# A conv-plus-linear-attention kernel: merged parameter loads, a shorter exponent matrix, a later zero-fill, and a new table for the order

## The chip, the cores and the metric

The kernel runs on one core of one Trainium2 chip. The metric is the device time of one execution in microseconds, lower is better. Engines are named as in the profile: TensorE (PE, with its weight loads as PEld), VectorE (DVE), ScalarE (ACT), GpSimd (POOL) and SyncE (SP), which here issues all DMAs.

## The reference

Two independent heads work on 2048 positions and 576 channels in float32; their results are joined along the last axis.

```python
# head A: long convolution with a kernel made of 128 damped waves per channel
dt = exp(log_dt);  A = -exp(log_A_real) + 1j * A_imag;  C = (C_real + 1j * C_imag) * dt[:, None]
P = exp((A * dt[:, None])[:, :, None] * pos)                  # (576, 128, 2048)
K = 2 * einsum("dn,dnl->dl", C, P).real                       # (576, 2048)
y = irfft(rfft(u.T, 4096) * rfft(K, 4096))[:, :2048].T + u * D_skip

# head B: linear attention, 32 heads of 18, with a learned feature map
q, k, v = split(x @ wqkv)
pq, pk = q @ w_phi, k @ w_phi                                 # per head
phi = lambda p: concat(softmax(p), softmax(-p))               # 36 features
o = phi(pq) @ (phi(pk).T @ v) / (phi(pq) @ sum(phi(pk)) + 1e-6)
b = o.reshape(2048, 576) @ wo
out = concat(y, b)
```

## The kernel before

**Head B.** 16 tiles of 128 positions. A key tile (`key_tile`) is three float32 products split into high and low parts (42 matmuls of 378 or 396 columns), a double softmax (`softmax`) and the keys-times-values product (32 matmuls `ps<-e,v`), which accumulates over the 16 tiles in `kvt`. The first of these products, of whichever tile comes first in the order, writes the mark `opened`; the others read it. After the last one the result is written into a block diagonal: `kvb` (126 x 1330) is cleared by GpSimd (L636) and stored to the DRAM buffer `kz` (L637), the 18 x 18 blocks are stored over it (L652), and the whole is loaded back into `kvb` (L655). Before that, `kvb` serves as a stage for one piece of the key weights. A query tile (`query_tile`) has a query product in two halves of 14 matmuls of 288 columns, softmax, ten transposes, the division (`ps<-kvb,fT`), transposes and the output product, again in two halves. The weights of keys and values are folded with `w_phi` on the chip (`fold`, `ps<-fT,e`), then those of queries (`fold` again) take their place.

**Head A.** 36 groups of 16 channels, done in pairs, in six blocks of six. For a block, `params` loads the step size `dt` (in `ldt`), the frequencies `th` and the two parts `cre` and `cim` of the coefficients, each 128 x 96, and works out phases in turns; `exponents` loads the block's exponents `mg` from the DRAM buffer `gd`, which `mags` has filled. `gd` holds 64 rows (four kinds times 16 channels). For a group, GpSimd builds integer phases by doubling (L883 to L888), ScalarE makes sines and cosines (L905 to L916), three matmuls with the constant `sel` (`ps<-sel,mg`) make exponents, ScalarE exponentiates them (L930), VectorE multiplies (L936 to L941) and 64 small matmuls (`ps<-E,cs`) give the kernel's rows. `sel` is loaded in three pieces (`sel_part`) through the buffer `v1`, of which there are two and which the key tiles use as well; every group's matmuls wait for all three. `mg` and `sel` have 128 rows: `mg` holds `gd` twice, and `sel` holds zeros where the second copy isn't wanted. Then the kernel (`k_first`, `ps<-ks,w`) and `u` (`u_first`, `ps<-ub,w`) go through a first transform stage to DRAM; 16 `product` steps (`ps<-ub,ff`, `ps<-kb,fk`, `ps<-ac,ff`) multiply them, and 16 `last` steps (`ps<-zi,w`) end the inverse transform.

**The order.** All operations are handed to `Plan.op`, and `Plan.run` writes them out engine by engine. It keeps a modelled time of each engine, and picks among the ready operations by a key: the due time in the table `WANT` (one number per unit, such as a key tile or a group pair), less the `LEAD` of the step. Operations given as `any` or as a pair of engines go to the one that the model has free first. Where the model sees TensorE wait for the first matmul into a fresh PSUM buffer, it writes fillers ahead (products with a zero tile, L215), which keep TensorE busy. SyncE's DMAs stand in one queue in the order of the plan. A `Mark` is a dependency without a buffer. `WANT`, `LEAD` and five weights are numbers in the file.

Of the kernel before, what the change touches and what calls it, by code (L numbers as in the profile page):

```python
# [8 lines left out]
F32 = mybir.dt.float32  # L9
# [13 lines left out]
NG, DG = 36, 4  # L23
# [18 lines left out]
def by_row(x):  # L42

    x = x.reshape(NQ, 4, NG // NQ, DG, -1).transpose(0, 2, 1, 3, 4).reshape(NG, W, -1)
    x = np.concatenate([x, np.repeat(x[-1:], 40 - NG, 0)])
    return np.ascontiguousarray(x.reshape(8, 5, W, -1).transpose(2, 0, 1, 3).reshape(128, -1))


def layouts(i):
    c = np.ascontiguousarray  # L50
    w = i["B_wqkv"]
    wphi = np.zeros((128, 5, 126), np.float32)
    h = 0
# [7 lines left out]
    return dict(  # L61
        u=c(i["A_u"][0].reshape(64, 16, 2, D).transpose(2, 0, 1, 3).reshape(128, 16 * D)), mag=np.stack([by_row(x) for x in (lar, cre, cim)]), ldt2=by_row(i["A_log_dt"][:, None]), aim=by_group(i["A_A_imag"]), cre=by_group(i["A_C_real"]),
        cim=by_group(i["A_C_imag"]), ldt=by_group(i["A_log_dt"][:, None])[0], dsk=c(i["A_D_skip"]),
        xT=twice(i["B_x"][0].T), wv=twice(w[:, 1152:]), wqT=c(twice(w[:, :576]).T), wkT=c(twice(w[:, 576:1152]).T), wphi=wphi,
        wo=twice(i["B_wo"]))


def constants():
# [83 lines left out]
class Mark(Buf):  # L152


    def __init__(self):
        self.tag, self.writers, self.readers = None, [], []


class Plan:
# [26 lines left out]
    def op(self, eng, cost, fn, r=(), w=(), with_=(), early=0.0, table=None, busy=1.0, lock=False, mode=(128, 128), add=None):  # L186
# [10 lines left out]
        for b in w:  # L197
            b.writers.append(k)
        bufs = list({id(b): b for b in (*r, *w, *with_) if not isinstance(b, Mark)}.values())
        for b in bufs:  # L200
# [175 lines left out]
def c_dma(nbytes, run=4096):  # L376
    return nbytes / run * (0.35 + 0.0029 * run)
# [4 lines left out]
FLEX = "dve", "pool"  # L382
STAY, TURNOVER, NEAR, LEAN_POOL, LEAN_ACT = 201.0337, 32.8045, 106.7441, -80.6454, 62.4245
LEAD = dict(g1=-171.8003, g2=572.2435, g3=151.3761, g4=545.6015, k1=48.5812, k2=-375.6500, k3=-757.7275, k4=-640.2771, l1=-1201.2185, p1=-789.5548, p2=-44.7091, p3=-18.2983, p4=-535.3487, q1=82.0847, q2=-177.3983, q3=-254.3079, q4=-403.9251, q5=-398.9575, q6=-829.6788, u1=458.1288, xd=-783.9802)
FILL = 114.0


WANT = dict(
    ident=[-108.8011],
    fold=[-9953.8356, -10398.4174, -453.1777, 165.8967],  # L390
    start=[1616.5931],
    key=[-6472.8031, -3126.8062, -1314.3574, -3125.3684, -656.72, -499.3546, -3140.1215, -1712.5806, -2108.3757,
          -1097.3828, -995.3063, -3475.5769, -5054.2771, -1149.402, -2645.614, -12059.5893],
    kv=[-10.1299],
    query=[5165.3029, 1080.554, 692.3202, 1735.0859, -197.7761, 3588.2092, 2132.912, 435.8626, 2776.5646, 4448.3212,
          4159.3881, 4303.4831, 5219.083, 4714.8471, 4446.1239, 3107.4294],
    u=[-1640.9461, -3267.9218, -4820.103, -2553.3502, -977.4058, -3531.8924, -390.5478, -577.8274, -2654.6962,
          -4160.3913, -2177.6267, -4468.1255, -741.7491, -4170.1538, -4622.046, -4241.0767],
    mags=[-9388.2816],
    sel=[-7210.3842, -4975.1123, -11383.6242],  # L400
    dsk=[2087.7151],
    par=[-11102.6929, -5509.5329, -1199.9769, -424.7275, 1524.2103, 2698.0598],
    group=[-7457.0019, -5406.6149, -4731.1573, -4251.2752, -3514.0599, -2749.8781, -3073.1041, -3256.4294, -3042.7242,
          -2141.1152, -1003.1983, -2662.6797, -315.8551, -156.0662, 211.9443, 4253.1033, 2854.2949, 574.2642],
    kfirst=[-4429.7629, -1297.4347, -385.4741, 1666.6694],
    product=[-90.1674, 1697.6391, -210.3218, 1304.2139, 977.2179, -172.77, 437.5617, -517.2988, 1754.78, 1904.223,
          3993.8576, 2617.1633, 3713.9029, 3193.0326, 3608.0088, 3162.4523],
    last=[2342.2332, 1752.2374, 2676.4796, 653.6455, 734.6483, 754.2121, 126.96, 2202.2106, 3127.1116, 3903.7028,
          3067.4349, 3943.3771, 2944.3536, 3914.8745, 4473.7986, 2888.4515],
)  # L410


def body(tc, nc, i, out, ctx):
# [9 lines left out]

    tags({1: "zero ident w1 w3 hp quarter dsk kvb fT wh wl ks E sel dt th cre cim ax ay mx mn ld ldc",
          2: "v1 o ot pi mg ff ub kb zo us2 ac yo zi", 3: "e fk x9", 4: "cs", 7: "small"})
# [209 lines left out]
    line = lambda: kvb.t.rearrange("p s k g d -> p (s k g d)")  # L635
    op("pool", 1400, lambda: pool.memset(line(), 0.0), w=[kvb])  # L636
    op("sp", c_dma(126 * 5320), lambda: sp.dma_start(flat(), line()), r=[kvb], w=[kz, blank])  # L637
# [127 lines left out]
    pl.at("mags")  # L765
    sel, ld, ldc = B("sel", [128, 1536], F32R), B("ld", [128, 5]), B("ldc", [128, 5])
# [32 lines left out]
    def sel_part(k):  # L799
        st = B("v1", [128, 512])  # L800
        cs = slice(k * 512, k * 512 + 512)
        op("sp", c_dma(128 * 2048), lambda: sp.dma_start(st.t, i["sel"][:, cs]), w=[st])
        copy("act", lambda: sel.t[:, cs], lambda: st.t, [st], [sel], 512)
# [4 lines left out]
    def exponents(blk):  # L808
        mg = B("mg", [128, NG // NB, NS], F32R)
        for h in range(2):  # L810
            op("sp", c_dma(64 * 3072), lambda h=h: sp.dma_start(
                mg.t[64 * h:64 * h + 64].bitcast(F32), gd.t[:, NG // NB * blk:NG // NB * (blk + 1)]), r=[gd], w=[mg])
        return mg

    def params(blk):
        cs = slice(blk * BW, blk * BW + BW)
        dt, th, cre, cim, ax, ay, mx, mn = (B(n, [128, BW]) for n in (
            "dt", "th", "cre", "cim", "ax", "ay", "mx", "mn"))
        tmp, at = dt, ax
        pi, fx = B("pi", [128, 12, BW]), B("ot", [128, 4, BW])  # L820
        op("sp", 300, lambda: sp.dma_start(dt.t, i["ldt"][cs].rearrange("(o d) -> o d", o=1).to_broadcast([128, BW])), w=[dt], early=8)
        for b, n in ((th, "aim"), (cre, "cre"), (cim, "cim")):
            op("sp", 300, lambda b=b, n=n: sp.dma_start(b.t, i[n][:, cs]), w=[b], early=8)

# [294 lines left out]
```

## Time and profile before

| | |
|---|---|
| median of 3 runs | 588.4 us (586.17 to 588.89) |
| profiled execution | 588.28 us, of which the span of the profile is 586.5 us |
| mean granted TensorE clock | 0.991 |
| TensorE busy | 556.6 us (95%) |
| VectorE busy | 513.1 us (87%) |
| ScalarE busy | 389.5 us (66%) |
| GpSimd busy | 251.8 us (43%) |
| DMA | 119.24 MB, queue share 65.1% of 16 engines |

Busy times are of one profiled execution. TensorE's busy time includes the fillers, and its matmuls overlap, so it is no measure of how much work there is.

### The profile page before, as it was taken

The page shows a single profiled execution, that of the slowest core. Times are in us where ns is not written, and L with a number is a line of the kernel's source. Part 1 is how long each engine was busy: PE and PEld are TensorE (multiplying, and loading weights), DVE is VectorE, ACT ScalarE, POOL GpSimd, SP SyncE. Part 2 cuts the span into 40 slices and gives each one's busy share as a digit, 9 for nine tenths or more (in the row PEclk, how much of TensorE's full clock was granted, in tenths as well). Part 3 has the DMA queues.
Part 4 walks back from the last instruction along what each step waited for, and adds up shares of the span by engine and source line. Part 5 has one row for each costly group of instructions (what it writes and reads, how often), then busy time and mean ns, then how long its engine had stood idle before and what let it go on. Part 6 is the DMA issues. An engine that isn't in the chain of part 4 may idle for free.

```text
span 586.5 us, 18741 instructions
## 1 busy us (share of the span) xinstructions
PE 556.6 (95%) x7657; PEld 457.9 (78%) x7657; DVE 513.1 (87%) x1109; ACT 389.5 (66%) x666; POOL 251.8 (43%) x393
## 2 busy tenths in 40 slices
PE   5998999999999899899999999999999999999996
PEld 3998989898879688778888766676788876767884
DVE  5789999999999899799999999799979797777751
ACT  5567767898579978578789777595955444432342
POOL 0448388682383656670566750674300201211000
PEclk9899999999999999899999999999999999999999
DMA  8977521457156767315867466975685799997587
GB/s 250 293 271 233 179 92 45 157 204 253 53 141 205 227 204 212 103 54 128 244 208 209 137 199 163 313 241 160 203 272 180 190 281 305 321 302 253 182 258 207
DMA packets 91316, 119.24 MB, mean 203 GB/s; under 512 B 9826, under 2 KB 73186, under 8 KB 91230
## 3 DMA queue, kind: packets, MB, share of 16 engines
q1 hardware_dynamic: 91230, 118.04, 65.1%
q8 instruction: 60, 0.98, 0.8%
q14 instruction: 26, 0.21, 0.1%
HBM read 68.76 MB, written 49.26 MB: 201 GB/s over the span
## 4 chain that ended last, share of the span: by engine, by line
PE 53%; DVE 24%; DMA 10%; ACT 5%; issue 3%; POOL 2%; SPq 2%; DVEq 0%; ACTq 0%; POOLq 0%
PE ps L431 49%; DVE E L937 3%; DVE e L446 3%; DMA zi<-dram 2%; DVE cs L936 2%; PE ps L678 2%; DMA out_dram<-yo 2%; DVE E L941 1%; DVE E L939 1%; DMA e<-in_wkT_dram 1%; DVE small L580 1%; DVE small L568 1%; PE ps L215 1%; DVE zi L436 1%; DVE e L450 1%
## 5 line engine op out<-in xcount | busy, mean ns | idle before, releaser
L431 PE MATMUL ps<-wh,x 128*128 128x288 f32 (+2 forms) x1008 | 241.8, 320 | 2.5 <-DVE zi L436 1.6
L431 PEld LDWEIGHTS ps<-wh,x 128*128 128x128 f32 x1008 | 174.2, 189 | 14.5 <-issue 6.7
L431 PE MATMUL ps<-wl,x 128*128 128x288 f32 (+2 forms) x560 | 175.5, 314 | 0.0
L888 POOL TENSOR_TENSOR cs<-cs,pi 128x32 int32<-128x32 int32 (+4 forms) x180 | 113.5, 639 | 9.4
L431 PEld LDWEIGHTS ps<-wl,x 128*128 128x128 f32 x560 | 106.4, 190 | 0.7
L579 POOL TENSOR_TENSOR o<-e 128x576 f32<-128x576 f32 x32 | 43.1, 1352 | 98.6 <-ACT e L576 77.1
L930 ACT ACTIVATE ps<-ps 128x512 f32<-128x512 f32 x108 | 56.6, 583 | 10.8 <-PE ps L431 9.7
L431 PEld LDWEIGHTS ps<-kvb,fT 126*128 126x128 f32 (+1 forms) x320 | 39.6, 192 | 8.8 <-issue 2.5
L450 DVE TENSOR_TENSOR ac<-us,ps 128x576 f32<-128x576 f32 x64 | 44.5, 743 | 1.4 <-ACT fT L436 1.1
L431 PE MATMUL ps<-E,cs 128*32 128x64 f32 x2304 | 42.4, 223 | 2.8 <-DVE E L941 1.8
L431 PE MATMUL ps<-kvb,fT 126*128 126x133 f32 (+1 forms) x320 | 42.8, 283 | 1.9 <-ACT fT L436 1.9
L431 PEld LDWEIGHTS ps<-E,cs 128*32 128x32 f32 x2304 | 35.6, 111 | 11.5 <-DVE E L941 4.1
L936 DVE TENSOR_TENSOR cs<-ps,cs 128x1024 f32<-128x1024 f32 x36 | 43.6, 1211 | 1.0 <-ACT ps L930 0.8
L937 DVE TENSOR_TENSOR E<-ps,cs 128x1024 f32<-128x1024 f32 x36 | 43.4, 1207 | 0.1
L446 POOL TENSOR_TENSOR ac<-ac 128x288 f32<-128x288 f32 x19 | 15.3, 805 | 65.2 <-DVE ac L450 65.1
L576 ACT ACTIVATE e<-e 128x1152 f32<-128x1152 f32 x32 | 37.4, 1179 | 5.4 <-POOL e L446 1.9
L436 ACT ACTIVATE ot<-ps 128x288 f32<-128x288 f32 x29 | 11.9, 416 | 40.8 <-PE ps L431 39.8
L912 ACT ACTIVATE cs<-cs 128x1040 f32<-128x1040 int32 x36 | 38.3, 1063 | 0.2
L431 PE MATMUL ps<-sel,mg 128*128 128x512 f32 x108 | 35.4, 428 | 2.8 <-ACT zi L436 1.7
L905 ACT ACTIVATE cs<-cs 128x1040 f32<-128x1040 int32 x31 | 33.1, 1070 | 5.7 <-POOL cs L888 5.7
L916 ACT ACTIVATE cs<-cs,hp 128x1040 f32<-128x1040 f32 x31 | 35.6, 1149 | 0.0
L431 PE MATMUL ps<-kb,fk 128*64 128x288 f32 x256 | 35.4, 414 | 0.1
(141 smaller groups left out, 1058.6 us busy)
## 6 DMA issues: line engine op xcount, KB each, us to landing
xd<-x SPq DMA_DIRECT2D x16, 576.0 KB
dram<-zi SPq DMA_DIRECT2D x16, 576.0 KB
dram<-zi SPq DMA_DIRECT2D x32, 288.0 KB
x<-xd SPq DMA_DIRECT2D x16, 576.0 KB
kb<-dram SPq DMA_DIRECT2D x32, 288.0 KB
ub<-dram SPq DMA_DIRECT2D x32, 288.0 KB
dram<-zo SPq DMA_DIRECT2D x32, 288.0 KB
zi<-dram SPq DMA_DIRECT2D x16, 576.0 KB
```

Source lines behind the costliest of these rows:

```text
L431: pe.matmul(o, l, r, start=start, stop=stop, skip_group_check=skip)
L446: op(eng, [c_dve(n[0]) if e == "dve" else c_pool(n[1]) for e in eng], lambda e: (dve if e == "dve" else pool).tensor_tensor(dst(), a(), b( ...
L450: op(eng, c_dve(n) if eng == "dve" else c_pool(n), lambda: e.tensor_tensor(dst(), a(), b(), op=alu), r=r, w=w, lock=eng == "pool" or not a ...
L576: op("act", c_act(1152) + 40, lambda: act.activation(e.t, e.t, AF.Exp), r=[e], w=[e], table="exp")
L579: op("pool", c_pool(470), lambda: pool.tensor_tensor(pair.t, e.t[:, :, :, 0:9], e.t[:, :, :, 9:18], op=ALU.add), r=[e], w=[pair], lock=True)
L888: op("pool", c_pool(2 * n * W), lambda n=n, j=j: pool.tensor_tensor(x()[:, :, :, n:2 * n], x()[:, :, :, 0:n], pi.t[:, j:j + 2, gs].bitcast ...
L905: act.activation(cs.t[:, 0], x(), AF.Abs)
L912: act.activation(cs.t[:, 1], cs.t[:, 1].bitcast(I32), AF.Sin, scale=TURN)
L916: act.activation(cs.t[:, 0], cs.t[:, 0], AF.Sin, scale=-TURN, bias=hp.t)
L930: op("act", c_act(512), lambda: act.activation(ps.t, ps.t, AF.Exp), r=[ps], w=[ps], table="exp")
L936: op("dve", c_dve(64 * W), lambda: dve.tensor_tensor(F(), both(M.t), F(), op=ALU.mult), r=[M, cs], w=[cs])
L937: op("dve", c_dve(64 * W), lambda: dve.tensor_tensor(E.t[:, :, :, 32:64], both(up.t), cs.t[:, :, :, 0:32], op=ALU.mult), r=[up, cs], w=[E])
```

## The change

1. The four parameter loads of a block become one load of 128 x 384 from an array `four` laid out for it. One buffer (`dt`, one copy) holds all four; `Part` is a mark that stands for a quarter of it, so that each step still waits for its quarter, while the buffer comes free after the last reader of any.
2. `gd` gets eight rows of zeros, written once by a DMA from the zero tile. `mg` and `sel` have 72 rows in place of 128, and a block's exponents are one load in place of two.
3. The memset of `kvb` reads the mark `opened`, so it and its store come after the first keys-times-values product.
4. All numbers of the planner's tables are others, so every engine's order is another. The matmuls other than fillers are the same ones; fillers are 207 in place of 193; ScalarE has 38 table loads in place of 34.

```diff
+    four = np.stack([np.repeat(by_group(i["A_log_dt"][:, None]), NS, 0)] + [by_group(i[x]) for x in ("A_A_imag", "A_C_real", "A_C_imag")])
+    four = c(four.reshape(4, NS, NB, BW).transpose(1, 2, 0, 3).reshape(NS, -1))
...
-    none = np.zeros_like(at)
-    sel = np.concatenate([np.concatenate([at, none, dn], 1), np.concatenate([none, up, none], 1)])
+    sel = np.concatenate([np.concatenate([at, up, dn], 1), np.zeros((8, 1536))])
...
+class Part(Mark):
+    def __init__(self, of, k):
+        super().__init__()
+        self.of, self.k = of, k
+    @property
+    def t(self):
+        return self.of.t[:, self.k]
...
-LEAD = dict(g1=-171.8003, g2=572.2435, g3=151.3761, g4=545.6015, k1=48.5812, ...
+LEAD = dict(g1=-596.9929, g2=367.2719, g3=-490.9828, g4=1181.4843, k1=316.9776, ...
...
-    op("pool", 1400, lambda: pool.memset(line(), 0.0), w=[kvb])
+    op("pool", 1400, lambda: pool.memset(line(), 0.0), r=[opened], w=[kvb])
...
-    gd = B("gd", [4 * W, 40, NS])
+    gd = B("gd", [4 * W + 8, 40, NS])
+    op("sp", 640 * 1.1, lambda: sp.dma_start(gd.t[64:72].rearrange("r g n -> (r g n)").rearrange("(p k n) -> p k n", p=128, k=5),
+                                              pl.zero.t.bitcast(F32)[:, None, :].to_broadcast([128, 5, 64])), r=[pl.zero], w=[gd])
...
-        st = B("v1", [128, 512])
+        st = B("v1", [72, 512])
...
-        mg = B("mg", [128, NG // NB, NS], F32R)
-        for h in range(2):
-            op("sp", c_dma(64 * 3072), lambda h=h: sp.dma_start(
-                mg.t[64 * h:64 * h + 64].bitcast(F32), gd.t[:, NG // NB * blk:NG // NB * (blk + 1)]), r=[gd], w=[mg])
+        mg = B("mg", [4 * W + 8, NG // NB, NS], F32R)
+        op("sp", c_dma(72 * 3072), lambda: sp.dma_start(mg.t.bitcast(F32), gd.t[:, NG // NB * blk:NG // NB * (blk + 1)]), r=[gd], w=[mg])
...
-        op("sp", 300, lambda: sp.dma_start(dt.t, i["ldt"][cs].rearrange("(o d) -> o d", o=1).to_broadcast([128, BW])), w=[dt], early=8)
-        for b, n in ((th, "aim"), (cre, "cre"), (cim, "cim")):
-            op("sp", 300, lambda b=b, n=n: sp.dma_start(b.t, i[n][:, cs]), w=[b], early=8)
+        four = B("dt", [128, 4, BW])
+        dt, th, cre, cim = (Part(four, k) for k in range(4))
+        op("sp", c_dma(128 * 1536, 1536), lambda: sp.dma_start(
+            four.t.rearrange("p k n -> p (k n)"), i["four"][:, 4 * BW * blk:4 * BW * (blk + 1)]), w=[dt, th, cre, cim], early=8)
```

What the new order looks like is shown at three places. First, SyncE's queue at the start of the program, before (`in_sel` is the first third of `sel`, `in_wv` and `in_wkT` are the value and key weights, `in_wphi` the feature map):

```order
L473 DMA zo<-in_xT_dram 128x5x128
L802 DMA v_97<-in_sel_dram 128x512
L821 DMA dt<-in_ldt_dram 128x96
L823 DMA th<-in_aim_dram 128x96
L823 DMA cre<-in_cre_dram 128x96
L823 DMA cim<-in_cim_dram 128x96
L473 DMA zi<-in_wv_dram 128x5x192 x2
L473 DMA cs<-in_wv_dram 128x5x192
L482 DMA fT<-in_wphi_dram 128x630
L486 DMA e<-in_wkT_dram 126x640 x2
```

and SyncE's queue at the same place now:

```order
L836 DMA dt<-in_four_dram 128x384
L487 DMA zo<-in_xT_dram 128x5x128
L487 DMA zi<-in_wv_dram 128x5x192 x2
L487 DMA cs<-in_wv_dram 128x5x192
L496 DMA fT<-in_wphi_dram 128x630
L500 DMA e<-in_wkT_dram 126x640 x2
L500 DMA E<-in_wkT_dram 126x640
```

The first key weights come after six issues in place of ten, and `sel` is no longer ahead of them.

Second, the zeroed block diagonal. GpSimd's queue around its memset before (`pi` are the first block's phases, `v1` a key tile's values, `x9` a key tile's input):

```order
L450 TENSOR_TENSOR pi_133<-pi_133 128x96
L450 TENSOR_TENSOR pi_133<-pi_133 128x192 x2
L636 MEMSET kvb_335 126x1330
L450 TENSOR_TENSOR pi_133<-pi_133 128x192
L615 MEMSET v1_345 128x32
L450 TENSOR_TENSOR pi_133<-pi_133 128x192
L446 TENSOR_TENSOR x9_343<-zo_168,x9_343 64x128
```

GpSimd's queue around it now (`cs_660` are the phases of the fourth group, `o` and `e` belong to a key tile's softmax):

```order
L902 TENSOR_TENSOR cs_660<-cs_660,pi_119 128x16x2x8
L629 MEMSET v1_783 128x32
L650 MEMSET kvb_791 126x1330
L902 TENSOR_TENSOR cs_660<-cs_660,pi_119 128x16x2x16
L593 TENSOR_TENSOR o_882<-e_621 128x576
L464 TENSOR_TENSOR pi_419<-pi_419 128x96
```

and SyncE's queue where its store now stands (`dt` is the third block's parameters, `v1_855` the last third of `sel`):

```order
L496 DMA fT_785<-in_wphi_dram 128x630
L836 DMA dt_801<-in_four_dram 128x384
L651 DMA kz_807<-kvb_791 126x1330
L818 DMA v1_855<-in_sel_dram 72x512
L760 DMA ub_875<-in_u_dram 128x576
L771 DMA dram_394<-zi_849 128x1152
```

The memset has moved from the first block's phases, ahead of all groups, to a place between the fourth group's doublings; the store has moved to the place directly ahead of the last third of `sel`.

Third, TensorE's queue behind the last group's matmuls (`E`), before (`wh` and `wl` are the query and output weights, `ks` the group's result that enters `k_first`):

```order
L431 MATMUL ps_7292<-E_7219,cs_6611 32x64 x32
L431 MATMUL ps_7330<-wh_3090,x9_7222 128x288
L431 MATMUL ps_7330<-wl_3091,x9_7222 128x288
L431 MATMUL ps_7330<-wh_3090,x9_7222 128x288 x2
L431 MATMUL ps_7330<-wl_3091,x9_7222 128x288
L431 MATMUL ps_7330<-wh_3090,x9_7222 128x288 x2
L431 MATMUL ps_7330<-wl_3091,x9_7222 128x288
L431 MATMUL ps_7330<-wh_3090,x9_7222 128x288 x2
L431 MATMUL ps_7330<-wl_3091,x9_7222 128x288
L431 MATMUL ps_7330<-wh_3090,x9_7222 128x288 x2
L431 MATMUL ps_7330<-wl_3091,x9_7222 128x288
L431 MATMUL ps_7350<-ks_5900,w1_253 64x288
```

and TensorE's queue there now (rows with `zero` are fillers, `ident,e` transposes of a query tile):

```order
L445 MATMUL ps_7298<-E_7242,cs_6842 32x64 x32
L229 LDWEIGHTS zero_81
L229 MATMUL ps_7344<-ident_99,zero_81 126x256
L229 LDWEIGHTS zero_81
L229 MATMUL ps_7344<-ident_99,zero_81 126x256
L692 MATMUL ps_7344<-ident_99,e_6703 126x128 x4
L445 MATMUL ps_7353<-ks_6133,w1_210 64x288
```

A half query tile stood behind the last group before; now two fillers and four transposes stand there. From that point to the end 24 such halves, 9 `last` steps and 12 fillers remain, in place of 25, 12 and none.

More of the change, by code (lines that the diff above doesn't have):

```diff
@@ L61, in layouts @@
     return dict(
[L62 to L63 removed]
+        u=c(i["A_u"][0].reshape(64, 16, 2, D).transpose(2, 0, 1, 3).reshape(128, 16 * D)), mag=np.stack([by_row(x) for x in (lar, cre, cim)]), ldt2=by_row(i["A_log_dt"][:, None]), four=four,
+        dsk=c(i["A_D_skip"]),
         xT=twice(i["B_x"][0].T), wv=twice(w[:, 1152:]), wqT=c(twice(w[:, :576]).T), wkT=c(twice(w[:, 576:1152]).T), wphi=wphi,
@@ L198, in op @@
             b.writers.append(k)
-        bufs = list({id(b): b for b in (*r, *w, *with_) if not isinstance(b, Mark)}.values())
+        parts = [b.of for b in (*r, *w) if isinstance(b, Part)]
+        bufs = list({id(b): b for b in (*r, *w, *with_, *parts) if not isinstance(b, Mark)}.values())
         for b in bufs:
@@ L385 @@
+LEAD = dict(g1=-596.9929, g2=367.2719, g3=-490.9828, g4=1181.4843, k1=316.9776, k2=-220.8799, k3=-2198.2025, k4=-520.6920, l1=-811.5782, p1=-279.5317, p2=-417.1315, p3=-485.8669, p4=-415.8287, q1=223.9279, q2=-289.5980, q3=-448.7975, q4=-502.1689, q5=-436.9106, q6=-997.3467, u1=740.1929, xd=-934.5048)
 FILL = 114.0
 WANT = dict(
[L389 to L393, printed above, removed]
@@ L408 @@
-    last=[2342.2332, 1752.2374, 2676.4796, 653.6455, 734.6483, 754.2121, 126.96, 2202.2106, 3127.1116, 3903.7028,
-          3067.4349, 3943.3771, 2944.3536, 3914.8745, 4473.7986, 2888.4515],
+    ident=[1246.8953],
+    fold=[-9373.4449, -11041.9236, -1452.2708, -738.1885],
+    start=[3762.3507],
+    key=[-7908.8211, -3217.3921, -2751.28, -1169.6395, -1541.4876, -1261.3998, -3829.9347, -13218.5904, -3590.9709,
+          -2456.9081, -4376.271, -2454.6704, -1838.419, -2340.4702, -2944.9904, -2655.4107],
@@ L422, in tags @@
                 pl.tag(t, p, n, window)
-    tags({1: "zero ident w1 w3 hp quarter dsk kvb fT wh wl ks E sel dt th cre cim ax ay mx mn ld ldc",
+    tags({1: "zero ident w1 w3 hp quarter dsk kvb fT wh wl ks E sel dt ax ay mx mn ld ldc",
           2: "v1 o ot pi mg ff ub kb zo us2 ac yo zi", 3: "e fk x9", 4: "cs", 7: "small"})
```

40 lines of the change are left out of this document (20 added, 20 removed).

## The prediction

> **What bounds the kernel now.** I read the page first, then the busy time by stretches, then the start, the first group and the end in the timeline. The head of the page:
>
> ```profile
> span 586.5 us, 18741 instructions
> PE 556.6 (95%) x7657; PEld 457.9 (78%) x7657; DVE 513.1 (87%) x1109; ACT 389.5 (66%) x666; POOL 251.8 (43%) x393
> ...
> PE 53%; DVE 24%; DMA 10%; ACT 5%; issue 3%; POOL 2%; SPq 2%; DVEq 0%; ACTq 0%; POOLq 0%
> ```
>
> The third line is the chain that ended last: TensorE holds half of it, VectorE a quarter. The busy times by stretch (start:end, length, then each engine's busy time and its number of instructions, the granted clock, the DMA share and GB/s):
>
> ```profile
> 0.00:30.00 30.00, 22.75 (x141) 20.64 (x142) 18.91 (x52) 16.79 (x31) 8.09 (x24) 0.89 0.92 274
> ...
> 60.00:120.00 60.00, 59.20 (x1094) 54.10 (x1093) 59.17 (x118) 45.30 (x70) 40.70 (x64) 1.00 0.38 121
> 120.00:180.00 60.00, 58.99 (x905) 51.31 (x905) 58.36 (x123) 46.83 (x73) 33.75 (x53) 1.00 0.50 155
> 180.00:225.00 45.00, 41.53 (x741) 34.23 (x738) 41.91 (x100) 40.93 (x67) 26.34 (x41) 1.00 0.71 218
> ...
> 330.00:360.00 30.00, 27.75 (x427) 19.72 (x423) 29.81 (x63) 23.76 (x37) 14.39 (x22) 1.00 0.58 170
> ...
> 453.00:560.00 107.00, 106.28 (x1253) 81.22 (x1253) 83.29 (x198) 40.61 (x93) 16.21 (x15) 1.00 0.84 262
> 560.00:586.50 26.50, 21.27 (x167) 17.37 (x165) 9.03 (x22) 7.66 (x18) 0.00 (x0) 1.00 0.78 236
> ```
>
> Three regimes are to be seen. In the first 30 us the DMA engines are 92% busy and TensorE is not. From 60 to 360 us VectorE and TensorE are both nearly full, so a wait on either shows in the other. From 453 us to 560 TensorE alone is full. 453 us is where the matmuls of the last (36th) convolution group stand:
>
> ```profile
> 453.04 1.10 PE L431 MATMUL ps<-E,cs 128*32 128x64 f32 x64
> ```
>
> The sum is made against the profiled execution's own 588.28 us, 1.8 us over its span and 0.02% below the median of 588.4.
>
> **The change part by part.** Every table of the planner is new, so the order of all engines is new, while the work is almost the same: TensorE has the same matmuls apart from its fillers (207 for 193). I go through the program from its start and cost what differs.
>
> *The first loads.* SyncE's issues (start, duration, issue), the first TensorE work, and the size of one load of `sel` and of one of the four parameters:
>
> ```profile
> 0.74 0.46 SPq L473 DMA_DIRECT2D zo<-in_xT_dram  x1
> 1.26 0.51 SPq L802 DMA_DIRECT2D v<-in_sel_dram  x1
> 1.81 0.43 SPq L821 DMA_DIRECT2D dt<-in_ldt_dram  x1
> ...
> 3.23 0.43 SPq L823 DMA_DIRECT2D cim<-in_cim_dram  x1
> 3.70 1.00 SPq L473 DMA_DIRECT2D zi<-in_wv_dram  x2
> ...
> 6.47 1.15 SPq L486 DMA_DIRECT2D e<-in_wkT_dram  x2
> 14.36 2.05 PE L431 MATMUL ps<-fT,e 126*128 126x126 f32 x8 [5.65 <-DMA e<-in_wkT_dram]
> ...
> v<-in_sel_dram SPq DMA_DIRECT2D x3, 256.0 KB
> dt<-in_ldt_dram SPq DMA_DIRECT2D x6, 48.0 KB
> ```
>
> The first key-weight product waits for its load from 6.47 to 14.36 us. Ahead of that load stand 256 KB of the first third of `sel` and four parameter loads. In the new order the `sel` load is gone from there and the parameters are one load of the same 4 x 48 = 192 KB. At the 274 GB/s of this stretch 256 KB are 0.96 us; the four issues less are (3.70 - 1.26) x 4/5 = 1.95 us. Since the queue is full, the bytes decide: I take -1.0, and keep 0 and -1.95. Cover: if the first product's weights become late for another reason, this gain is gone and costs nothing.
>
> *The parameters.* ScalarE is their first reader, six blocks in all (count | busy, mean ns | idle before, released by):
>
> ```profile
> L827 ACT ACTIVATE ax<-cre 128x96 f32<-128x96 f32 x6 | 1.7, 281 | 4.7 <-DVE pi L450 3.7 <-DMA cre<-in_cre_dram 1.0
> L827 ACT ACTIVATE dt<-dt 128x96 f32<-128x96 f32 x6 | 1.7, 280 | 2.4 <-DMA dt<-in_ldt_dram 2.4
> L827 ACT ACTIVATE ay<-cim 128x96 f32<-128x96 f32 x6 | 1.7, 279 | 0.6 <-DMA cim<-in_cim_dram 0.5
> L431 PE MATMUL ps<-sel,mg 128*128 128x512 f32 x108 | 35.4, 428 | 2.8 <-ACT zi L436 1.7 <-DVE zi L436 0.6 <-ACT v L436 0.5
> ```
>
> ScalarE stood idle 1.0 + 2.4 + 0.5 = 3.9 us for these loads. One load leaves one wait. The merged tile comes free only after its last reader, which is true of `dt` already (it is also the scratch tile), so the wait for `dt` may stay; I take away the other two, -1.5, and keep 0 and -3.9. The 22 SyncE rows fewer and the 56 partitions fewer of `sel` and `mg` I cost at nothing: SyncE's queue is 2% of the chain, and the matmuls of `sel` and `mg` (last row) waited 2.8 us in all, mostly for copies of `zi` and not for a load; if that cover fails it is one issue of about half a microsecond per block.
>
> *The zeroed block diagonal.* Before, it is cleared and stored near 25 us, when GpSimd is nearly idle; now both stand behind the first keys-times-values product. The places there:
>
> ```profile
> 61.62 0.75 PE L431 MATMUL ps<-e,v 128*19 128x36 f32 x64
> 62.41 0.33 SPq L802 DMA_DIRECT2D v<-in_sel_dram  x1
> 65.47 0.63 ACT L439 ACTIVATE sel<-v 128x512 fp32r<-128x512 f32 x1 [0.43 <-DMA v<-in_sel_dram]
> 68.20 0.86 PE L431 MATMUL ps<-sel,mg 128*128 128x512 f32 x3
> ...
> L636 POOL MEMSET kvb<- 126x1330 f32 x1 | 1.2, 1212 | 0.3 <-PE ps L431 0.3
> kz<-kvb SPq DMA_DIRECT2D x1, 654.6 KB
> ```
>
> The last third of `sel` is issued when the first product ends, is copied by 66.1 us, and the first group's matmul comes at 68.20: 2.1 us of slack. Now SyncE issues the 654.6 KB store directly ahead of that load, and the store waits for the memset, which waits for the product. The memset (1.2 us) holds up GpSimd's queue, whose next two rows are the last doubling of a group's phases and a softmax sum. The bytes are 2.4 us at 274 GB/s, and the issue is 0.4 us. Against the slack I charge +0.5; the ends are 0 and 2.4 + 0.4 + 1.2 - 2.1 = +1.9, or all of the first three, +4.0, if the slack is gone. The store that leaves the full DMA queue at 25 us could give up to the same 2.4 us back; I count 0, since 19 fillers (20 before) still stand ahead of the second key product.
>
> *Up to the last group.* Counting each program's rows up to the 36th group and pricing them by their shapes:
>
> ```profile
> L436 DVE COPY zi<-ps 128x288 f32<-128x288 f32 x62 | 25.2, 444 | 4.9 <-PE ps L431 4.7
> L436 ACT ACTIVATE zi<-ps 128x288 f32<-128x288 f32 x66 | 23.2, 421 | 13.1 <-PE ps L431 11.3 <-ACT fT L436 0.9 <-ACT cs L905 0.4
> L912 ACT ACT_TABLE_LOAD x14 | 18.0, 1283 | 0.2
> ```
>
> VectorE has 6 copies of 288 columns fewer (6 x 25.2/62 = 2.4 us) and about 1.1 us less of the rest: -3.5. ScalarE has 15 such copies more (15 x 23.2/66 = 5.3 us), four table loads more (5.1 us) and some 11 us of other work, 21 us in all. VectorE is 97 to 99% busy in 60:180 and 330:360, less elsewhere, so I count half of its 3.5: -1.7 (ends -3.5 and 0). ScalarE has a quarter of its time free before the last group (389.5 - 40.6 - 7.7 = 341 us busy of 453), but carries 5% of the chain: 21 x 5% = +1.0 (ends 0 and the table loads' 5.1).
>
> *After the last group.* Here TensorE is full, so its own rows are the time:
>
> ```profile
> 533.12 0.38 PE L431 MATMUL ps<-wh,x 128*128 128x288 f32 x1
> ...
> 535.15 1.20 PE L431 MATMUL ps<-ub,ff 64*32 64x288 f32 x32
> ...
> 450.00 1.25 PE L678 MATMUL ps<-ident,e 128*126 128x128 f32 x10
> 207.41 1.59 PE L215 MATMUL ps<-ident,zero 128*32 128x256 bf16 x13
> L431 PE MATMUL ps<-zi,w 128*64 128x288 f32 x128 | 18.3, 415 | 1.2 <-DMA zi<-dram 1.1
> ```
>
> In the new order one half-tile query product (2.0 us from 533.12 to 535.15) and three of the 16 last-stage steps (18.3/16 = 1.1 us each) less stand behind the group, one set of transposes (1.25) and 12 fillers (12 x 1.59/13 = 1.5) more: -2.0 - 3.4 + 1.25 + 1.5 = -2.7. This is only won if the work moved ahead found room there; half-sure, I keep 0 as the other end.
>
> *The clock in the middle.*
>
> ```profile
> 240.00:245.00 5.00, 3.77 (x66) 3.64 (x70) 2.23 (x7) 2.36 (x4) 3.28 (x2) 0.68 0.33 115
> 241.23 2.44 PE L431 MATMUL ps<-kvb,fT 126*128 126x133 f32 x12 [1.95 <-ACT fT L436]
> ```
>
> Around the first query division TensorE ran at 0.68 for 5 us, a loss of 1.6 us, after idle pieces of which the longest is 1.95 us. The new order puts 57 fillers (7.0 us) shortly ahead of that division. If they keep the clock up, -1.6; I count 0, because they also occupy TensorE. The Trainium skill, in "TensorE: Matmul & The Clock Gate", Part 1 on the HAM clock gate, has the clock halve only after an idle window of about 3.4 us. By that page this dip should not have come from a 1.95 us gap, and fillers would win nothing there; by the row they could win 1.6 us and the sum would be 581.3. The trace does not agree with the page's window here.
>
> The sum: 588.28 - 1.0 - 1.5 + 0.5 - 1.7 + 1.0 - 2.7 = 582.9 us.
>
> **The rivals.**
>
> *TensorE is the whole bound.* Then what is moved ahead of the last group is paid there, VectorE's gain is idle, and only the start and the 14 fillers more count: 588.28 - 1.0 + 14 x 1.59/13 (1.7) = 589.0. For it: 95% busy. Against it: TensorE's busy time includes 193 fillers, and VectorE holds 24% of the chain.
>
> *ScalarE becomes the bound, slower.* In 180:225 it is busy 40.93 of 45 us, 4.1 us free. By the 18th group (which ends in or shortly after that stretch) the new order has given it about 10.8 us more. If that falls there, the excess of 10.8 - 4.1 = 6.7 us is on the path in place of +1.0, VectorE's 1.7 is idle, and the last group comes late, so that the 2.7 us at the end are lost: 588.28 - 1.0 - 1.5 + 0.5 + 6.7 = 593.0. It decides from more than 4.1 us of added ScalarE work within that stretch. Against it: the work is added over 250 us, most of which have a quarter free.
>
> *The store delays the first group.* The full +4.0 in place of +0.5: 582.9 + 3.5 = 586.4. For it: the store, the memset and the load form a line on one queue. Against it: more `u` products now lie before the first group and can fill the gap.
>
> **How the numbers follow.** The forecast has 0.50 (its own range, by its bounds, 577 to 588), TensorE alone 0.18, ScalarE 0.22, the store 0.10. The low end: all good bounds, 588.28 - 1.95 - 3.9 - 3.5 - 2.7 - 1.6 = 574.6, is reached only together; I take 576. The high end is the slower rival and a little, 594. A measurement of this kernel can tell about 0.5%, 2.9 us, from no change: faster is under 585.4, slower over 591.3. Faster: 0.43 of the forecast's 0.50, 0.03 of TensorE's, 0.02 of ScalarE's and 0.03 of the store's, 0.51. Slower: 0.18 of ScalarE's, 0.05 of TensorE's and 0.04 of the store's and the forecast's together, 0.27. Same: 0.22.
>
> **What would show it.** Right: the first key-weight product near 13.4 us instead of 14.36; no wait for `cre` or `cim` on ScalarE; the first group's matmul at or before 68 us; the last group's matmuls at or before 452 us; less than 133 us from there to the end. Wrong: the last third of `sel` landing late behind the store; ScalarE 98% busy anywhere between 180 and 330 us with VectorE waiting for its exponentials; TensorE idle after 453 us for loads of the last stage; a clock below 0.9 in a stretch that has none now.

## The result and the profile after

Slower by 1.1%: 594.42 us (median of 4, 593.68 to 596.74) against 588.18 us of before (median of 4, 586.17 to 588.89), ratio 1.0111, interval 1.0079 to 1.0143. The profiled execution of after took 594.67 us, against 588.28. One execution of the experiments below (596.85 us, with the first run opened) was in a slower state and is left out of its median. Head of the page of after (span, busy times, chain that ended last):

```profile
span 592.9 us, 18704 instructions
PE 563.2 (95%) x7671; PEld 460.3 (78%) x7671; DVE 507.4 (86%) x1088; ACT 398.1 (67%) x687; POOL 257.8 (43%) x397
...
PE 68%; DVE 12%; DMA 7%; issue 4%; ACT 3%; POOL 3%; SPq 1%; DVEq 0%; ACTq 0%; POOLq 0%
```

TensorE's share of the chain went from 53% to 68%, VectorE's from 24% to 12%: VectorE has its 5.7 us less, and nothing came of it. Busy times of after by stretch, in the columns of the table before; the last two begin at its own last group:

```profile
0.00:30.00 30.00, 23.06 (x143) 20.21 (x144) 20.17 (x55) 17.68 (x33) 3.50 (x15) 0.89 0.88 269
...
120.00:180.00 60.00, 55.59 (x924) 50.15 (x923) 53.74 (x101) 45.09 (x67) 35.80 (x50) 0.97 0.29 84
180.00:225.00 45.00, 41.76 (x724) 33.40 (x722) 41.15 (x81) 31.53 (x60) 21.65 (x33) 0.93 0.69 218
...
459.00:566.00 107.00, 106.45 (x1260) 82.20 (x1254) 83.25 (x192) 38.07 (x93) 11.77 (x12) 1.00 0.77 234
566.00:592.90 26.90, 20.00 (x147) 14.91 (x145) 7.55 (x17) 7.17 (x15) 1.32 (x1) 0.96 0.78 239
```

In 120:180 TensorE lost 3.4 busy us (58.99 before) and VectorE 4.6 (58.36), in the stretch where both were full; from 120 to 225 the granted clock is no longer 1.00. Three places on TensorE (start, duration):

```profile
13.57 2.05 PE L445 MATMUL ps<-fT,e 126*128 126x126 f32 x8 [5.18 <-DMA e<-in_wkT_dram]
...
65.76 1.20 PE L445 MATMUL ps<-sel,mg 72*128 72x512 f32 x3 [0.29 <-ACT v L450]
...
459.08 1.06 PE L445 MATMUL ps<-E,cs 128*32 128x64 f32 x58
```

The first key-weight product is 0.8 us and the first group's matmul 2.4 us earlier. The last group's matmuls end at 459.08 + 1.06 = 460.14 instead of 453.04 + 1.10 = 454.14. So everything is lost between the first group and the last. TensorE's waits of after have a row with no releaser, which before has not (total, times, longest), and the timeline shows the two places:

```profile
PE ps L445 <- issue: 5.5, 2, 3.7
```

```profile
157.16 1.38 PE L445 MATMUL ps<-e,v 128*19 128x36 f32 x127
...
158.37 0.72 PE L445 MATMUL ps<-E,cs 128*32 128x64 f32 x34
162.80 0.64 PE L445 MATMUL ps<-E,cs 128*32 128x64 f32 x28 [3.71 <-issue]
...
211.87 0.72 PE L445 MATMUL ps<-e,v 128*19 128x36 f32 x62
...
212.51 1.25 PE L229 MATMUL ps<-ident,zero 128*32 128x256 bf16 x10
...
213.72 1.28 PE L445 MATMUL ps<-E,cs 128*32 128x64 f32 x55
216.79 0.30 PE L445 MATMUL ps<-E,cs 128*32 128x64 f32 x3 [1.80 <-issue]
```

Twice TensorE stops in the middle of one group's 64 matmuls. Such a group waits for its operands at two places, ahead of its first matmul and after 8 of them, and both stops come later. At the first place two keys-times-values products (V) and a group (E) stand in a row, 192 matmuls of 36 or 64 columns; it stops after 164. At the second it is V, 12 fillers and E, and the stop comes 3 matmuls before the end. In before, V and E stand in a row of 128 at most. Behind both stops the granted clock drops:

```profile
160.00:165.00 5.00, 2.20 (x35) 2.11 (x36) 0.92 (x5) 1.51 (x4) 1.25 (x5) 0.90 0.20 76
165.00:170.00 5.00, 5.00 (x93) 3.72 (x92) 3.77 (x8) 2.93 (x7) 3.00 (x4) 0.76 0.29 120
215.00:220.00 5.00, 3.21 (x16) 1.87 (x17) 2.89 (x9) 2.37 (x6) 2.45 (x7) 0.86 0.25 67
220.00:225.00 5.00, 5.00 (x24) 4.03 (x20) 4.41 (x7) 2.65 (x7) 0.93 (x1) 0.50 0.85 326
```

My theory: TensorE runs out of instructions in a dense run of small matmuls, and these stops cost the time. Rivals: one of the three parts costs it, or the new order does, but through ScalarE and fillers.

### The profile page after: what moved, and what is told of

It reads as the page before. It is cut to its first block, busy times and chain, and to the rows that moved or that the text cites. A ratio compares the mean times of both kernels' runs of the same rounds, so it can differ in the third digit from the quotient of the medians.

```text
span 592.9 us, 18704 instructions
## 1 busy us (share of the span) xinstructions
PE 563.2 (95%) x7671; PEld 460.3 (78%) x7671; DVE 507.4 (86%) x1088; ACT 398.1 (67%) x687; POOL 257.8 (43%) x397
## 4 chain that ended last, share of the span: by engine, by line
PE 68%; DVE 12%; DMA 7%; issue 4%; ACT 3%; POOL 3%; SPq 1%; DVEq 0%; ACTq 0%; POOLq 0%
PE ps L445 63%; DMA zi<-dram 4%; PE ps L692 2%; DVE cs L950 2%; DMA e<-in_wkT_dram 1%; DVE e L460 1%; PE ps L229 1%; POOL wl L528 1%; DVE E L951 1%; DMA mg<-gd 1%; PE ps L720 1%; DMA v<-in_sel_dram 1%; DVE ac L464 1%; POOL cs L902 1%; DVE small L582 1%
## 5 line engine op out<-in xcount | busy, mean ns | idle before, releaser
L902 POOL TENSOR_TENSOR cs<-cs,pi 128x32 int32<-128x32 int32 (+4 forms) x180 | 117.8, 658 | 9.7
L460 POOL TENSOR_TENSOR ac<-ac 128x288 f32<-128x288 f32 x21 | 17.6, 838 | 54.0 <-DVE ac L464 54.0
L582 DVE TENSOR_REDUCE small<-ps 128x16 f32<-128x288 f32 (+2 forms) x64 | 28.8, 450 | 12.7 <-PE ps L445 12.3
L445 PE MATMUL ps<-sel,mg 72*128 72x512 f32 x108 | 36.9, 439 | 0.3 <-ACT v L450 0.3
L897 POOL MEMSET cs<- 128x16 f32 x36 | 4.6, 127 | 74.1 <-PE ps L445 68.0
```

The lines of the kernel that those rows point to most:

```text
L445: pe.matmul(o, l, r, start=start, stop=stop, skip_group_check=skip)
L460: op(eng, [c_dve(n[0]) if e == "dve" else c_pool(n[1]) for e in eng], lambda e: (dve if e == "dve" else pool).tensor_tensor(dst(), a(), b( ...
L582: op("dve", c_dve(DH * m), lambda: dve.tensor_reduce(ends.t[:, :, 0], v(), axis=AX.X, op=ALU.max, negate=True), r=[p], w=[ends])
L902: op("pool", c_pool(2 * n * W), lambda n=n, j=j: pool.tensor_tensor(x()[:, :, :, n:2 * n], x()[:, :, :, 0:n], pi.t[:, j:j + 2, gs].bitcast ...
```

## The experiments

All kernels below but after replay a recorded order, so that an edit moves only what is named. "Old order" is that of before, "new order" that of after. Medians in us; the ratio is to before in the same session (588.18 us for after; 588.84, 587.64 and 587.61 in the three sessions of the experiments). It stands with its 95% interval and is not exactly the quotient of the medians. Where two kernels of different sessions are compared, the ratios are the safer guide, since before itself moved by up to 1.2 us.

| kernel | median | ratio, interval |
|---|---|---|
| after | 594.42 | 1.0111 (1.0079 to 1.0143) |
| new order, both dense runs opened | 587.17 | 0.9965 (0.9934 to 0.9996) |
| new order, first run opened | 588.75 | 1.0023 (0.9991 to 1.0055) |
| new order, 12 fillers left out | 591.69 | 1.0072 (1.0045 to 1.0098) |
| old order, all three parts | 598.18 | 1.0157 (1.0118 to 1.0196) |
| old order, merged load alone | 595.51 | 1.0127 (1.0101 to 1.0153) |
| old order, 72 rows and late zero-fill | 586.92 | 0.9984 (0.9961 to 1.0007) |
| old order, all parts, two buffers | 587.71 | 0.9994 (0.9976 to 1.0013) |
| new order, old parts | 597.11 | 1.0152 (1.0106 to 1.0198) |
| opened, four parameter loads | 593.46 | 1.0117 (1.0079 to 1.0156) |
| opened, without 57 fillers | 585.08 | 0.9954 (0.9930 to 0.9977) |
| opened and trimmed | 586.78 | 0.9981 (0.9959 to 1.0002) |
| old order, five groups repeated (one execution) | 617.21 | none |

**The dense runs opened.** TensorE's queue of after (V9 is key tile 9's keys-times-values product, E9 the ninth group's 64 matmuls):

```diff
+V9
 396-column product of key tile 12
-V9
 V11
 E9
...
+V3
 ten key-weight products
-V3
-12 fillers
 E11
```

> The kernel after with three edits on TensorE's queue alone: one keys-times-values product goes ahead of the 396-column product before it, another goes ahead of ten of the key-weight products before it, and the 12 fillers ahead of that group are left out, so that no more than 128 small matmuls stand in a row. Theory A: no stop without a releaser behind 130 us, the granted clock stays at 1.0 behind 163 and 217 us, and 586 to 590 us in all (5.5 us of stops, and up to 6 of clock behind them, where TensorE is what is waited for). Rival C: the stops may go, the time stays at 593 to 595.

587.17 us, 7.2 below after. No wait without a releaser is left, and the clock is 1.00 in every 60 us from 60 to 540. The last group's row, and the stretches behind it:

```profile
449.70 0.99 PE L545 MATMUL ps<-E,cs 128*32 128x64 f32 x56 [0.23 <-DVE E L1076]
```

```profile
449.60:557.00 107.40, 105.33 (x1240) 81.52 (x1242) 82.05 (x190) 36.99 (x89) 11.80 (x12) 1.00 0.75 231
557.00:587.20 30.20, 22.83 (x157) 16.98 (x153) 8.82 (x21) 8.06 (x17) 1.31 (x1) 0.88 0.72 216
```

It ends at 450.69, 9.45 us earlier than in after: the stops' 5.5, the 12 fillers (12 x 1.59/13 = 1.5, at most), and some 2.5 left, for which the lower clock behind the stops is the candidate: in after it stands at 0.50 for 3.41 us from 164.00 and for 10.24 us from 218.61, at most 6.8 us of TensorE's time. ScalarE's queue and all others are the same in both kernels, so the rival of ScalarE falls too. The 12 fillers were part of the edit and are taken alone below.

**One run at a time.** The first edit alone, then only the fillers removed:

```diff
+V9
 396-column product of key tile 12
-V9
```

> The kernel after with one edit: one keys-times-values product goes ahead of the 396-column product before it, so that the run of 192 small matmuls at 157 us is 128 long. The run at 212 us stays. With both runs opened the time was 587.2 us, against 594.4 of the kernel after. If the stops themselves are what costs (3.7 us and 1.8 us, and the 12 fillers of the second place about 1.5): 590 to 592 us, no stop near 159 us and one of 1.5 to 2 us near 211. If the granted clock behind the stops costs as much again: 588 to 590.

```diff
-12 fillers
 E11
```

> The kernel after with one edit: the 12 fillers between the keys-times-values product and the group at 212 us are left out, so that this run is 128 small matmuls long instead of 140, with ten products of 126 columns ahead of it. The run of 192 at 157 us stays with its stop. If a run of 128 is short enough, as in the kernel before: no stop near 216 us, one of 3.5 to 4 us near 159, and 591.5 to 593.5 us. If the products of 126 columns count as well: a stop of 1 to 2 us stays there, and 593 to 594.5.

588.75 with the first run opened; a stop of 1.67 us remained at 210 us. With only the fillers left out, 591.69: the first stop remained (3.40 us), the second run, now 128 long and cut by a wait of 0.80 us for its operands, went through; a stop of 0.60 us came 2 us later. By the ratios the first run costs 0.9% (5.2 us, with a stop of 3.71) and the second 0.4 to 0.6% (2.3 to 3.4 us, with a stop of 1.80 and at most 1.5 of fillers): both stops are paid about in full. 588.75 lies in the range that was expected if the clock behind the stop costs as well, but the spread is wide (586.20 to 594.53), so the split between stop and clock is rough.

**The dose.** In the kernel before, the matmuls of five groups are issued again:

```diff
-        op("pe", 910, f, r=[E, cs], w=[ps], with_=[ks], ...
+        times = AGAIN.get((g // 2, 28 + 12 * (g % 2)), 1)   # 2, 2, 3, 4, 6 for five groups
+        op("pe", 910, lambda: [f() for _ in range(times)], r=[E, cs], w=[ps], with_=[ks], ...
```

> The kernel before, with the 64 small matmuls of five groups issued several times in a row (same values again, so the output is the same): group 14 (the one with a keys-times-values product right behind) twice, 192 in a row with that product; groups 19, 21, 25 and 29 two, three, four and six times, which is 128, 192, 256 and 384 in a row. Theory A (TensorE runs out of instructions in a dense run): no stop at 128, a stop of 1.8 to 4 us without a releaser after 130 to 170 matmuls at 192 and 256, and two at 384. Rival: if the stops came from something else at those places of the new order, such as a load or a wait that the records leave out, the runs of 192 to 384 go through at 16 to 25 ns each. The time itself says little here: about 12 us of work more.

TensorE's timeline at the five places (128 in place of 64 with V behind; 128; 192; 256; 384):

```profile
215.02 2.00 PE L545 MATMUL ps<-E,cs 128*32 128x64 f32 x128
216.83 0.44 PE L545 MATMUL ps<-e,v 128*19 128x36 f32 x28
220.66 0.79 PE L545 MATMUL ps<-e,v 128*19 128x36 f32 x36 [3.39 <-issue]
...
297.92 1.99 PE L545 MATMUL ps<-E,cs 128*32 128x64 f32 x128
...
318.06 2.31 PE L545 MATMUL ps<-E,cs 128*32 128x64 f32 x147
321.30 0.87 PE L545 MATMUL ps<-E,cs 128*32 128x64 f32 x45 [0.94 <-issue]
...
337.38 3.77 PE L545 MATMUL ps<-E,cs 128*32 128x64 f32 x255
342.60 0.22 PE L545 MATMUL ps<-E,cs 128*32 128x64 f32 x1 [1.44 <-issue]
...
394.54 3.37 PE L545 MATMUL ps<-E,cs 128*32 128x64 f32 x225
401.13 4.53 PE L545 MATMUL ps<-E,cs 128*32 128x64 f32 x159 [3.22 <-issue]
```

128 in a row pass, all four longer runs stop once, after 156, 147, 255 and 225 matmuls. So the length of the run makes the stop, in a kernel that had none. Not all came as expected: two stops are shorter than 1.8 us (0.94 and 1.44), two come later than after 170 matmuls, and the second stop at 384 did not come (behind its stop that run is slower, 28 ns each, at a granted clock of 0.50). The one execution took 617.21 us, 28 more than before; the four stops are 9.0 of that.

What TensorE lacks in a stop can be read from the DMA packets. One queue, of the kind `instruction`, brings packets of 16 KB (packets, MB, share of 16 engines; in before, then in this kernel):

```profile
q8 instruction: 60, 0.98, 0.8%
...
q8 instruction: 66, 1.08, 0.7%
```

Six packets more came for 6 x 128 = 768 matmuls more, so these are TensorE's instructions, and one packet serves about 128 matmuls with their weight loads (7657/60 = 127.6). In after, such a packet runs from 160.44 to 161.46 us, inside the first stop (159.09 to 162.80), and one from 214.57 to 215.49, across the start of the second (214.99 to 216.79). In these and all other stops of runs longer than 128, ten in five traces, TensorE goes on 1.26 to 1.56 us after such a packet has landed. So it is the supply of instructions that runs out. Why it does so there is only estimated: 128 of these matmuls last 1.4 to 2.0 us (157.16 in after, 297.92 here), while from a packet's start to TensorE's next matmul it was 2.2 to 3.1 us in the ten stops, so a long run can use instructions up faster than they come. How many are in store when a run begins is not in the records, which may be why the number at which it stops is not fixed.

**The parts without the order, and the order without the parts.**

```diff
 # parts as in after
-order of after
+order of before   (merged loads where the first of the four stood; memset and store as early as the mark allows)
```

> The three parts of the change (one parameter load, 72 rows and zero rows, late zero-fill) in the order of the kernel before: every engine's queue is held as it was, only the loads that merge and the memset with its store stand elsewhere. Theory A (the new order costs the time, above all two stops of TensorE inside dense runs of small matmuls, and the parts are as small as predicted): 584 to 588 us, ratio 0.993 to 1.000. Rival B (a part costs it: the store behind the first keys-times-values product, or the one buffer for four parameters): 592 to 595 us. Rival C (only the new order costs, but through ScalarE and the fillers, not through the stops): 584 to 588 as in A.

```diff
-four=True, short=True, late=True
+four=False, short=False, late=False   (order of after)
```

> The parts of before (four loads, 128 rows with two loads, zero-fill without the wait) in the order of the kernel after. Theory A and rival C: 594 to 597 us, ratio 1.010 to 1.015, with the two stops of TensorE at about 159 and 215 us. Rival B: 586 to 590.

This I had not expected: the parts in the old order cost 9.3 us (598.18, above even rival B's range), with no stop over 0.3 us, and the old parts in the new order are no better than after (2.7 us slower by the medians, but the intervals overlap). Its stops were 3.31 and 0.31 us. So a part costs in the old order what it does not cost in the new one. In the first kernel ScalarE shows why; its queue, SyncE's issue, and ScalarE's waits for that load in the whole program:

```profile
289.85 0.38 ACT L550 ACTIVATE ks<-ps 128x256 f32<-128x256 f32 x1
296.59 0.28 ACT L962 ACTIVATE ay<-dt 128x96 f32<-128x96 f32 x1 [6.36 <-DMA dt<-in_four_dram]
...
290.91 1.69 SPq L951 DMA_DIRECT2D dt<-in_four_dram  x1
...
L962 ACT ACTIVATE ay<-dt 128x96 f32<-128x96 f32 x6 | 1.7, 276 | 12.4 <-DMA dt<-in_four_dram 6.4 <-DVE small L682 6.0
L962 ACT ACTIVATE ax<-dt 128x96 f32<-128x96 f32 x6 | 1.6, 273 | 5.8 <-DMA dt<-in_four_dram 5.8
```

The one buffer came free only after the block's last reader, the load was issued at 290.91, and ScalarE, which reads `cim` and `cre` next in this order, stood until 296.59 with everything behind it. It waits 6.4 + 5.8 = 12.2 us for that load in all, against 3.9 us for the separate ones in before.

**Which part it is.**

```diff
-four=True, short=True, late=True
+four=True, short=False, late=False   (order of before)
```

> Of the three parts only the merged parameter load, in the order of the kernel before (128 rows, two exponent loads and the early zero-fill stay). With all three parts in that order ScalarE waited 1.7 + 4.1 + 6.4 us for the merged load and the time rose by 9 us. Theory M (the one buffer for four parameters comes free only after the last reader of any of them, and in this order ScalarE reads the next block soon after): 594 to 599 us, with the waits of ScalarE for that load adding up to 8 to 13 us. Rival N (the 72 rows or the late zero-fill carry the 9 us): 586 to 590.

```diff
-four=True, short=True, late=True
+four=False, short=True, late=True   (order of before)
```

> The other two parts (72 rows with one exponent load, zero rows by DMA, late zero-fill) in the order of the kernel before, with four parameter loads in four buffers. Theory M: 586 to 590 us, as before, with the third copy of the constant matrix waiting at most 2 us behind the store. Rival N: 593 to 598.

```diff
-1: "... dt ...",  7: "small"
+2: "dt ...",      5: "small"       (all three parts, order of before)
```

> All three parts in the order of the kernel before, but two buffers for the merged parameters instead of one (the room is taken from the tag of small tiles, 5 in place of 7, of which that order never holds more than 5). Only SyncE's queue changes: each merged load is issued earlier. Theory M: ScalarE's waits for the merged load fall from 12 us to under 3, and the time to 585 to 590 us. Rival (the size of one load of 192 KB, or the other parts): stays at 594 to 598.

595.51, 586.92 and 587.71: the merged load alone costs 7.9 us, the other two parts nothing that can be told (-0.7), and a second buffer takes the whole cost away. With the merged load alone ScalarE waits 11.8 + 4.7 = 16.5 us for it, more than the 8 to 13 expected; not all of that shows in the time. With two buffers its only row of such waits is:

```profile
L962 ACT ACTIVATE dt<-dt 128x96 f32<-128x96 f32 x6 | 1.7, 280 | 0.7 <-DMA dt<-in_four_dram 0.7
```

The load is the same 192 KB, so neither its size nor its being one load matters: what matters is when its only buffer comes free.

**The merged load in the new order.** Both runs opened, then:

```diff
-four=True, short=True, late=True
+four=False, short=True, late=True   (order of after, both runs opened)
```

> The kernel after with both dense runs opened, but four parameter loads in four buffers instead of the merged one (72 rows and the late zero-fill stay). The prediction gave the merged load -1.0 us at the start and -1.5 us in ScalarE's waits: 588.5 to 590 us if that holds in this order. In the order of before the merged load cost 8 us; if it costs here too: 582 to 586.

593.46 against 587.17, so here the merged load earns 6.3 us by the medians and 1.5% by the ratios, more than the 2.5 us of the sum. SyncE's queue and ScalarE with four loads, then with the merged one:

```profile
97.33 0.33 SPq L955 DMA_DIRECT2D dt<-in_ldt_dram  x1
...
99.20 0.38 SPq L587 DMA_DIRECT2D zo<-in_xT_dram  x1
...
104.92 0.74 ACT L639 ACTIVATE x<-zo 128x640 fp32r<-128x640 f32 x1 [2.56 <-DMA zo<-in_xT_dram]
```

```profile
93.94 0.33 SPq L951 DMA_DIRECT2D dt<-in_four_dram  x1
94.37 0.40 SPq L587 DMA_DIRECT2D zo<-in_xT_dram  x1
...
98.86 0.74 ACT L639 ACTIVATE x<-zo 128x640 fp32r<-128x640 f32 x1
```

A key tile's input stands behind the parameters in SyncE's queue: 1.87 us behind the first issue with four, 0.43 with one, and ScalarE waits 2.56 us for it or not at all. The start of the program has the same: with four issues in place of one ahead of it, the first key-weight product comes at 13.98 instead of 12.58, and the first group's matmuls end 3.4 us later (75.45 instead of 72.08). Part of that may be chance, since after, also with one load, has 13.57 and 72.86. The fourth group's end 6.5 us later (113.37 instead of 106.88), of which 4.1 are left at the last group (454.79 instead of 450.69). In the order with both stops less of it shows: all the old parts together were 2.7 us slower there, within the intervals, with a second stop that was 1.5 us shorter.

**Fillers and clock.** Two more edits of the opened kernel:

```diff
-57 fillers
 E13
```

> The kernel after with both dense runs opened (587.2 us), and without the 57 fillers ahead of the thirteenth group (6.3 us of TensorE, in which it waits for that group's exponentials anyway). If the fillers only keep the clock up and the clock matters there: a granted clock of 0.6 to 0.8 in the 5 us behind 236 us and 588.5 to 590 us. If the clock there does not decide: the same dip, and 586 to 587.5 us. If they overrun the wait (they end 0.7 us after the group's last operand): 586.5 us.

```diff
-57 fillers
+50 fillers
 E13
...
-store of the zeroed block diagonal
 last third of sel
+store of the zeroed block diagonal
```

> The kernel after with both dense runs opened, 50 fillers in place of 57 ahead of the thirteenth group, and the store of the zeroed block diagonal behind the load of the last third of the constant matrix. The fillers overran by 0.7 us, the third waited 0.6 us: 585.5 to 587 us, and below before by 0.4 to 0.6% if the two small edits are worth what the trace shows; no more than both edits at nothing, 587.2.

Without the 57 fillers TensorE stands 6.05 us and the clock falls (with them it is 1.00 there):

```profile
235.18 0.44 PE L545 MATMUL ps<-E,cs 128*32 128x64 f32 x8 [6.05 <-DVE E L1074]
```

```profile
230.00:235.00 5.00, 0.00 (x0) 0.00 (x0) 4.22 (x9) 4.99 (x7) 1.04 (x1) 0.75 0.21 87
235.00:240.00 5.00, 4.66 (x76) 3.92 (x77) 4.66 (x8) 2.77 (x5) 4.79 (x7) 0.57 0.01 3
```

585.08 us, below all three ranges: the dip came and cost nothing that shows. The group waits for its exponentials either way, and the last group ends at 450.19 us, against 450.69 with the fillers. This is the fastest kernel of the study, 0.46% below before (0.23 to 0.70%); its interval overlaps that of the kernel with the fillers, so what the fillers cost (2.1 us by the medians, 0.6 by the ratios) may be nothing. The two trims moved nothing that can be told (586.78, and 0.2% below before instead of 0.4 to 0.6%).

## Why the prediction was wrong, point by point

The forecast was 582.9 us, in a range of 576 to 594, and 594.42 was measured: 6.2 us above before, not 5.4 below it.

- **The first loads** (-1.0): right, -0.8 at the first key-weight product.
- **The parameters** (-1.5): right in after (its waits for the load are 1.8 us against 3.9), but with the issues it saves the load was mis-sized in both directions. The SyncE rows fewer that I cost "at nothing" (23 by the traces, 395 issues against 372, not 22; 18 of them are the parameters') had delayed a critical input, so the merged load earns 4 to 6 us in this order with the runs opened; and I named the later release of the one buffer without asking which order pays it: in the old one it costs 8.
- **The zeroed block diagonal** (+0.5): it cost no more than that. The first group's matmul waits 0.29 us for a copy, not for `sel`, and in the old order the late zero-fill and the 72 rows moved nothing that can be told (-0.7). The rival of the store falls.
- **Up to the last group** (-1.7 and +1.0): VectorE's 5.7 us less are there. ScalarE's excess up to the last group is 11.6 us (398.1 - 38.07 - 7.17 = 352.9 busy against 341.2), not the 21 that I counted, and it is not in 180:225 (31.53 us busy against 40.93). So the ScalarE rival falls: that its 593.0 lies near the measured 594.4 is a coincidence, since edits of TensorE's queue alone took 7.2 us away. With the runs opened, the last group ends 454.14 - 450.69 = 3.45 us earlier; the sum had -2.7 up to there. **The step that failed** is "the work is almost the same: TensorE has the same matmuls apart from its fillers". I costed where TensorE's matmuls stand at nothing. Two dense runs, in which TensorE ran out of instructions, cost 9.45 us by the last group in the profiled executions (7.2 by the medians), and turned -3.45 into +6.0.
- **After the last group** (-2.7): wrong too, but smaller. From the last group to the end of the span it is 592.9 - 460.14 = 132.8 us, against 586.5 - 454.14 = 132.4. The half tile and the three last-stage steps moved ahead lower TensorE's busy time there by about 1.1 us and not by the 2.7 that I added up, and the end waits: in the last 26.9 us TensorE is idle 6.9, against 5.2 of 26.5 before. I priced by TensorE's rows a stretch whose end it does not set. That the stretch stayed under 133 us, a sign of being right, says nothing, since before was under 133 as well.
- **The clock in the middle** (0): right to count nothing, as the run without fillers shows. But the clock fell elsewhere, to 0.50, after idle pieces as short as the 1.95 us of the prediction's row: 1.80 us in after, 1.67 us with the first run opened. The Trainium skill, "TensorE: Matmul & The Clock Gate", Part 1 on the HAM clock gate, asks for an idle window of about 3.4 us; the traces do not agree with it here either.
- **TensorE the whole bound** (589.0): its mechanism was nearest, since what TensorE lost was paid in full around 160 and 215 us; but it lost by stops, which that rival did not have.

With both runs opened the kernel is faster than before by 0.35% (587.17, interval 0.9934 to 0.9996), which is still above the 585.4 that the prediction set for "faster". What is missing to 582.9 lies behind the last group, where the profiled execution of that kernel took 587.2 - 450.69 = 136.5 us, with a clock of 0.88 in the last 30. Without the 57 fillers the same stretch took 583.0 - 450.19 = 132.8. Why it is longer in the one execution than in before and after stays open.

## What to carry to other kernels

When a change reorders a queue, look not only at what is in it but at what stands side by side: count small matmuls in a row, and look for waits without a releaser inside one operation. The packets of the kind `instruction` tell whether such a stop is a wait for code. When loads are merged into one buffer, ask when its last reader is done and who reads first next, since the same merge cost 8 us in one order and earned 6 in another. Undo a change's parts with the order held; a change with a new order has no price apart from it.

## What the runs showed of the hardware

A run of 128 small matmuls (36 or 64 columns, each with its own weight load, 0.75 to 1.10 us for 64) passed wherever it stood. The ten runs of 140 to 384 stopped once each, after 136 to 255 matmuls, for 0.31 to 3.71 us, with no releaser in the records, and went on 1.26 to 1.56 us after a 16 KB packet of instructions had landed. The run of 140 has 12 fillers in it; without them, and cut by a wait of 0.80 us, it did not stop. Five stops of 0.28 to 0.63 us, in larger matmuls 2 to 5 us behind a run of 128, ended 1.21 to 1.51 us after such a packet.

The granted clock fell to 0.50 after idle pieces of 1.67, 1.80 and 2.08 us (three kernels), while in before one of 1.74 us at 195 us left it at 1.00. The dips lasted 3.41 us or a multiple of it (3.41 us at 164.00 and 10.24 us at 218.61 in after). Executions at a lower mean clock were mostly the longer ones of their kernel: with the first run opened, 593.30 to 594.53 us at 0.984 to 0.986 and 586.20 to 591.74 us at 0.991 to 0.996. Which of the two makes the other is not shown, and the trimmed kernel has no such order.
